# A banded attention and feed-forward kernel: the third tile's attention values in runs of two steps, the order of the work made anew, and the ring's buffers numbered by place

## The chip, the core and the metric

The kernel runs on one core of one Trainium2 chip. The metric is the time of one execution on the device, in microseconds; the number given for a kernel is the median of its runs. The core has five engines that matter here, each with a queue of instructions of its own: TensorE (PE, matmuls into PSUM), VectorE (DVE), ScalarE (ACT), GpSimd (POOL) and SyncE (SP), which issues nearly all the DMA transfers. An instruction waits at the head of its queue until what it needs is there, and everything behind it on that queue waits with it. So the order in each queue matters as much as what is computed.

## The reference

Attention over 8 x 8 heads, 576 positions and head size 64, in which a position sees only the 64 positions that end with itself; then its output, as 4608 tokens of 512 features, goes through a feed-forward layer of 2048 hidden features.

```
scores = scale * q @ k.T
mask = (rel >= 0) & (rel < window)          # rel = query position - key position, window 64
attn = softmax(where(mask, scores, -1e9))
x = (attn @ v), heads side by side           # [4608, 512]
h = x @ w_in                                 # [4608, 2048]
g = where(h >= 1, h, where(h <= -1, 0, (h + 1) ** 2 / 4))
out = g @ w_out                              # [4608, 512]
```

All of it is float32. A large matmul is made of three, each number being split in a high part and a rest: high by high, rest by high, high by rest.

## The kernel before, in words

**Tiles.** The 4608 tokens are 9 tiles of 512. The first three (PLAIN = 3) are computed directly: for each of 16 slices f of 128 hidden features, `ffn_in` (line 933) makes h in 12 matmuls, the activation follows, and `ffn_out` (line 984) adds to the output in 12 matmuls. The other six tiles form three supers of two tiles. For a super, the first layer is done with seven products in place of eight (the table PARTS, after Strassen), for eight groups n of two slices each: `ffn_product` (line 862) is 6 matmuls, and the results are put together in the h tiles by `h_copy` (line 280 in the profile, the common copy) and `h_add` (line 877). The sums of weights for the products are made once, kept in DRAM (`kept`), and loaded again for each product into a ring of six buffers (`ring_load`, line 843). In the first half of a super the first tile's outputs are made beside the products; the second tile's h goes out to DRAM (`spill`, line 880) for six of the eight groups and comes back (line 884) in the second half, where only outputs are made.

**The activation** of one slice is five instructions on tiles of 128 x 512: relu on ACT (line 946), square on ACT or DVE (lines 951 and 953), the gate on DVE (line 958: min with 1, max with h, both inputs in SBUF where h comes from the h tiles), the cast to the high part on ACT (line 963), and the low part on DVE or POOL (line 968). The pools of `a`, `gh` and `gl` have two buffers each. Outputs that have been summed up are copied and stored (line 1013); two of the four stores of a super's first tile go out from an h tile (`out<-h`), since the h tile is free by then.

**Attention** is 36 steps of 128 tokens. Each has scores on TensorE (line 425) into the two banks of the PSUM pool ps_a, mask and scale (442), maximum (446), exponential (453), inverse (460, 461), normalisation (465) and transposes (472), and then values on TensorE (line 507), which are split into xh (282 or 280) and xl (520). In the supers the values of two steps are one run into both banks of ps_a. In the third plain tile, steps 8 to 11, the scores of a step and the values of the step before it are one piece of work on TensorE, the values into a bank of ps_h. That piece is named `joined` in the code.

**What sets the order.** Class Plan is a list scheduler that runs while the program is written. Every piece of work has a key, a cost in ns per engine that may do it, what it needs, and which buffers of which pool it takes and gives back. At each step, each engine looks at what could start within PATIENCE ns of its earliest, and takes the smallest key of that; the earliest start over the engines is then written. Costs and keys come from a table of numbers at the head of the file. Work marked `shared` on DVE and all work on POOL are kept apart in the plan (`held`). The plan isn't what the chip does: it only fixes which instruction stands behind which on each queue, and, where two engines may do a piece, which of them does.

## Time and profile before

| what | value |
|---|---|
| time, median of 3 runs | 871.41 us (871.04 to 872.35) |
| the profiled execution | 871.15 us, span 869.4 us |
| granted TensorE clock | 1.00 |
| matmuls | 6718 |
| HBM read / written | 112.86 MB / 33.55 MB |

The span goes from the first to the last thing that the profiler saw; the execution's time has 1.75 us more around it. Rows of a group read: line, engine, operation, output <- inputs, shape, count, then busy time in us and mean ns of one, then how long the engine was idle just before such instructions and what ended that. Rows of a timeline read: start in us, length in us, engine, line, operation, count, and in brackets an idle time with what ended it. A matmul's end is modelled, so that single ones seem to overlap with the next; starts are what counts. The trace counts each matmul of scores and values twice (x64 and x32), where the order has 32 and 16.

### The profile page before, as it was taken

To read this page: it belongs to the slowest core of one execution; us is meant where nothing else is said; L and a number is where in the kernel's file an instruction comes from. 1 tells how busy PE (TensorE), PEld (TensorE's weight loads), DVE (VectorE), ACT (ScalarE), POOL (GpSimd) and SP (SyncE) were. 2 spreads that over 40 slices of the span, in tenths; PEclk is the share of its full clock that TensorE was granted. 3 is DMA by queue.
4 is the path that set the end of the run, shared out by engine and by line. 5 is a ranking of instruction groups with operands and counts; after the bars stand their busy time and mean duration, and the time that the engine had idled before them with its cause. 6 is when DMAs were issued, how large, how long until landed. Compare 5 with 4: busy or idle time off the path is not lost.

```text
span 869.4 us, 17790 instructions
## 1 busy us (share of the span) xinstructions
PE 857.3 (99%) x6718; PEld 699.7 (80%) x6718; DVE 652.2 (75%) x1260; ACT 490.5 (56%) x1236; POOL 208.7 (24%) x230
## 2 busy tenths in 40 slices
PE   8899999999999999999999999999999999999998
PEld 6788888888788887777878888888888888888786
DVE  6999995989887868888878969877789734343452
ACT  6999966556664566433447755343457633322564
POOL 1000045557542732131214001222141011111000
PEclk9999999999999999999999999999999999999999
DMA  8992126768644215766664418666544054635221
GB/s 317 413 393 77 49 80 217 218 184 250 195 161 142 83 37 176 243 207 194 196 205 135 176 43 267 204 197 212 171 134 146 25 177 145 194 126 182 74 97 48
DMA packets 88373, 147.58 MB, mean 170 GB/s; under 512 B 7776, under 2 KB 36704, under 8 KB 88288
## 3 DMA queue, kind: packets, MB, share of 16 engines
q1 hardware_dynamic: 87856, 145.40, 51.1%
q8 instruction: 53, 0.87, 0.4%
q10 hardware_dynamic: 432, 1.05, 0.4%
q14 instruction: 32, 0.26, 0.1%
HBM read 112.86 MB, written 33.55 MB: 168 GB/s over the span
## 4 chain that ended last, share of the span: by engine, by line
PE 91%; DVE 4%; DMA 3%; ACT 1%; issue 1%; SPq 0%; ACTq 0%
PE acc L984 44%; PE ps_h L862 24%; PE ps_h L933 15%; PE ps_a L425 3%; PE ps_a L507 3%; DMA raw<-in_w 2%; DVE ptd L472 1%; DVE h L877 1%; DMA kt<-in_k 1%; ACT sm L453 1%; DVE a L958 1%; PE ps_h L507 0%; PE ps_a L493 0%; DVE a L953 0%; DVE nm L446 0%
## 5 line engine op out<-in xcount | busy, mean ns | idle before, releaser
L984 PE MATMUL acc<-wts,gh 128*128 128x512 f32 x1152 | 358.2, 392 | 0.0
L984 PEld LDWEIGHTS acc<-wts,gh 128*128 128x128 f32 x1152 | 213.9, 188 | 45.9 <-issue 0.3
L984 PE MATMUL acc<-wts,gl 128*128 128x512 f32 x576 | 224.5, 390 | 0.0
L968 POOL TENSOR_TENSOR gl<-a,gh 128x512 fp32r<-128x512 f32 (+1 forms) x81 | 104.6, 1292 | 400.9 <-ACT gh L963 316.1
L862 PE MATMUL ps_h<-wts 128*128 128x512 f32 x720 | 182.3, 393 | 0.7 <-DVE h L877 0.5
L862 PEld LDWEIGHTS ps_h<-wts 128*128 128x128 f32 x720 | 133.4, 188 | 32.5 <-DVE h L877 3.8
L472 DVE STREAM_TRANSPOSE ptd<-sm 32x256 f32<-32x256 f32 x336 | 146.4, 436 | 7.8 <-PE ps_a L507 1.6
L946 ACT ACTIVATE a<-h 128x512 f32<-128x512 f32 x96 | 60.6, 632 | 136.2 <-DVE h L877 98.7
L877 DVE TENSOR_TENSOR h<-h,ps_h 128x512 f32<-128x512 f32 x120 | 82.3, 685 | 70.4 <-PE ps_h L862 66.8
L933 PE MATMUL ps_h<-xh,wts 128*128 128x512 f32 (+1 forms) x424 | 129.7, 374 | 1.3 <-DVE a L958 0.9
L984 PEld LDWEIGHTS acc<-wts,gl 128*128 128x128 f32 x576 | 108.1, 188 | 23.0 <-DVE gl L968 0.2
L453 ACT ACTIVATE sm<-sm,nm 128x96 f32<-128x96 f32 (+1 forms) x256 | 93.1, 366 | 41.0 <-DVE nm L446 40.9
L963 ACT CAST gh<-a 128x512 fp32r<-128x512 f32 (+1 forms) x149 | 89.3, 600 | 47.6 <-DVE a L958 27.4
L958 DVE SCALAR_TENSOR_TENSOR a<-a,h 128x512 f32<-128x512 f32 x96 | 79.4, 827 | 29.4 <-ACT a L951 27.4
L933 PEld LDWEIGHTS ps_h<-xh,wts 128*128 128x128 f32 x424 | 77.4, 188 | 16.8 <-DVE a L958 1.3
L933 PE MATMUL ps_h<-xl,wts 128*128 128x512 f32 (+1 forms) x212 | 78.5, 370 | 0.6 <-DVE xl L520 0.6
L951 ACT ACTIVATE a<-a 128x512 f32<-128x512 f32 (+1 forms) x121 | 74.4, 615 | 3.6
L862 PE MATMUL ps_h<-xs,wts 128*128 128x512 f32 x288 | 73.9, 392 | 0.1
L862 PEld LDWEIGHTS ps_h<-xs,wts 128*128 128x128 f32 x288 | 53.7, 188 | 11.9 <-ACT h L280 0.5
L280 ACT COPY h<-ps_h 128x512 f32<-128x512 f32 x42 | 24.6, 586 | 68.3 <-PE ps_h L862 68.2
L968 DVE TENSOR_TENSOR gl<-a,gh 128x512 fp32r<-128x512 f32 (+1 forms) x68 | 45.0, 663 | 8.9 <-ACT gh L963 8.0
L946 ACT ACTIVATE a<-ps_h 128x512 f32<-128x512 f32 (+1 forms) x53 | 29.3, 553 | 33.4 <-PE ps_h L933 32.2
(108 smaller groups left out, 856.7 us busy)
## 6 DMA issues: line engine op xcount, KB each, us to landing
wts<-kept SPq DMA_DIRECT2D x168, 256.0 KB, 3.0
vt<-in_v SPq DMA_DIRECT2D x72, 256.0 KB, 3.7
kt<-in_k SPq DMA_DIRECT2D x35, 384.0 KB, 4.3
raw<-in_w SPq DMA_DIRECT2D x12, 1023.8 KB, 10.2
qt<-in_q SPq DMA_DIRECT2D x36, 256.0 KB, 3.3
spill<-h SPq DMA_DIRECT2D x18, 512.0 KB, 3.0
h<-spill SPq DMA_DIRECT2D x18, 512.0 KB, 3.6
out<-o SPq DMA_DIRECT2D x27, 256.0 KB, 2.6
```

The lines of the kernel that those rows point to most:

```text
L425: nc.tensor.matmul(banks[h][r, p, :n], lhsT=qt[half[h], p, r], rhs=kt[half[h], p, i * m:i * m + n], start=not masked, stop=not masked or p ...
L453: nc.scalar.activation(sm[:, p, :], (ps if masked else sm)[:, p, :], AF.Exp, bias=nm[:, p:p + 1], scale=scale if masked else 1.0, accum_ou ...
L472: nc.vector.transpose(dst[:, :, r], src[:, :, c * SQ:(c + 1) * SQ])
L862: nc.tensor.matmul(ps, lhsT=r[:, part, cp], rhs=x_op(k, xp)[:, cp], start=j in (0, 1, 3, 4) and i == 0 and cp == 0, stop=j in (1, 2, 5, 6) ...
L877: nc.vector.tensor_tensor(out=h[:, to], in0=h[:, of], in1=prods[u, n, b], op=ALU.add)
L933: nc.tensor.matmul(ps, lhsT=wts[f, 0][:, part, c * P:(c + 1) * P], rhs=x[:, c, r], start=(c == 0 and j == 0), stop=(c == NP - 1 and j == 2),)
L946: nc.scalar.activation(gs[t, f, r.start][0], phs[t, f, r.start], AF.Relu, bias=0.5, scale=0.5)
L951: nc.scalar.activation(a, a, AF.Square)
L958: nc.vector.scalar_tensor_tensor(out=a, in0=a, scalar=1.0, in1=ps, op0=ALU.min, op1=ALU.max)
L963: nc.scalar.copy(g[1], g[0])
L968: engine[eng].tensor_tensor(out=g[2], in0=g[0], in1=g[1].bitcast(F32), op=ALU.subtract)
L984: nc.tensor.matmul(acc[t, i], lhsT=g[:, sub], rhs=wts[f, 1][:, part], start=(q == 0 and j == 0), stop=(q == NF - 1 and j == 2),)
```

## The change

Three things are changed.

First, in the third tile the scores of a step stand alone on TensorE, and the values of two steps (8 and 9, 10 and 11) are one run into both banks of ps_a, as the supers already do it. The `joined` pieces and the dictionary that carried them are gone. One flag, `paired`, now says for every step whether it waits for the next or ends a pair.

Second, the table has new numbers: keys of attention (B_DUE, B_STEP, B_FIRST, A_END, A_SUPER), of the products and outputs (C_STEP, Q_STEP, O_AFTER, O_LATER, O_CHANGE, G_LEAD, B_LATER), of the weights' sums (S_LATE, S_LATER, S_PACE), of reloads (R_LEAD, H_LEAD), of building the supers' inputs (BUILD), two costs (VV_PE, TURN) and POOL's PATIENCE.

Third, `ring_load` numbers the ring's buffers by a product's place i in the order, not by the product j. The two differ where LAST_PARTS swaps two products, in the last group of each super.

```
-PATIENCE = dict(ACT=300, DVE=0, Pool=404, PE=0, SP=0)
+PATIENCE = dict(ACT=300, DVE=0, Pool=176, PE=0, SP=0)
...
-G_LEAD = -1.3
-B_LATER = 6.43
+G_LEAD = -3.65
+B_LATER = 9.9
...
-        joined = SOON <= s and i < TILES[t] // SB - 1 and t < PLAIN
+        paired = (i < 4, i >= 4) if t >= PLAIN else (i % 2 == 0, i % 2 == 1) if s >= SOON else (False, False)
...
-        if before:
-            sv, (needs_v, gives_v, split) = before.popitem()
-
-            def do(e):
-                att_scores(s, masked, ps)
-                att_values(sv, "ps_h")
-
-            xs = add(
-                key, dict(PE=B_PE), do, needs + needs_v, takes=[ps, ps, "sm", "ps_h"],
-                gives=[("qt", xq), ("kt", xk)] + gives_v,
-            )
-            split(xs, key, "ps_h")
-        else:
-            xs = add(
...
+        xs = add(
+            key, dict(PE=S_LATER_PE if s >= SOON else S_PE[near(s)] + 500 * masked), lambda e: att_scores(s, masked, ps), needs,
+            takes=[ps, ps, "sm"], gives=[("qt", xq), ("kt", xk)],
+        )
...
-            x = add(due, dict(DVE=608), lambda e: att_low(t, i), [x], gives=[(pv, xo, t >= PAIRED and i >= 4)])
+            x = add(due, dict(DVE=608), lambda e: att_low(t, i), [x], gives=[(pv, xo, paired[1])])
...
-        if joined:
-            before[s] = needs, gives, split
-        elif t >= PAIRED and i < 4:
+        if paired[0]:
             waiting[s] = needs, gives, split
-        elif t >= PAIRED:
+        elif paired[1]:
...
-            xo = add(key, dict(PE=2 * V_LATER_PE - 91), both, needs0 + needs, takes=[pv, pv], gives=gives0 + gives)
+            xo = add(key, dict(PE=VV_PE), both, needs0 + needs, takes=[pv, pv], gives=gives0 + gives)
...
-    def ring_load(u, n, j):
-        m = 7 * (n + u * NF // 2) + j
+    def ring_load(u, n, i, j):
+        m = 7 * (n + u * NF // 2) + i
```

The numbers of instructions are the same on TensorE (5079 in both, the first difference at the 990th, which starts at about 163 us); on DVE, 28 squares become 11 (on ACT 111 become 128), and 62 low parts of 128 x 512 become 64 (on POOL 77 become 75). The changed file's lines are 15 lower from the products on: line 946 is 931 there, 951 is 936, 963 is 948, 884 is 869, 1013 is 998, 933 is 918, 984 is 969.

ACT's queue in the last super, in the first half, at about 800 to 812 us of the profile before. The numbers behind the names tell tiles apart: `a_8619` is the activation of one slice, and its cast is the row that reads it.

```order
L946 ACTIVATE a_8619<-h_4243 128x512
L963 CAST gh_8629<-a_8565 128x512
L946 ACTIVATE a_8664<-h_4243 128x512
L951 ACTIVATE a_8664<-a_8664 128x512
L963 CAST gh_8683<-a_8619 128x512
L280 COPY h_4244<-ps_h_8675 128x512 x2
L946 ACTIVATE a_8719<-h_4244 128x512
L963 CAST gh_8728<-a_8664 128x512
L946 ACTIVATE a_8753<-h_4244 128x512
```

The same place after the change:

```order
L931 ACTIVATE a_8621<-h_4200 128x512
L936 ACTIVATE a_8621<-a_8621 128x512
L948 CAST gh_8639<-a_8567 128x512
L931 ACTIVATE a_8666<-h_4200 128x512
L936 ACTIVATE a_8666<-a_8666 128x512
L948 CAST gh_8685<-a_8621 128x512
L280 COPY h_4201<-ps_h_8677 128x512 x2
L931 ACTIVATE a_8719<-h_4201 128x512
L936 ACTIVATE a_8719<-a_8719 128x512
L948 CAST gh_8736<-a_8666 128x512
```

Before, every other slice has its square on DVE, and there the cast of the slice before follows the relu at once; after, each relu is followed by its square on ACT, and the cast comes behind both.

SyncE's queue at the start of the first super's second half, at about 474 to 493 us before. `h_4243` and `h_4244` are the two h tiles (hA0 and hB0 in the first, hA1 and hB1 in the second), `out_0` is the output, `vt` are attention's values.

```order
L884 DMA h_4243<-spill2_101 128x1024
L403 DMA vt_5730<-in_v 128x512
L1013 DMA out_0<-o_5723 128x512
L1013 DMA out_0<-h_4244 128x512
L403 DMA vt_5757<-in_v 128x512
L403 DMA vt_5778<-in_v 128x512
L1013 DMA out_0<-h_4244 128x512
L884 DMA h_4244<-spill3_102 128x1024
L403 DMA vt_5806<-in_v 128x512
L884 DMA h_4244<-spill1_100 128x1024
L884 DMA h_4243<-spill4_103 128x1024
```

The same place after the change:

```order
L869 DMA h_4200<-spill2_101 128x1024
L998 DMA out_0<-o_5728 128x512
L998 DMA out_0<-o_5736 128x512
L998 DMA out_0<-h_4201 128x512
L403 DMA vt_5779<-in_v 128x512
L869 DMA h_4201<-spill3_102 128x1024
L998 DMA out_0<-h_4201 128x512
L869 DMA h_4201<-spill1_100 128x1024
L869 DMA h_4200<-spill4_103 128x1024
```

The second store from the h tile stood ahead of the reload of spill3 and stands behind it now; the reload of spill1, which fills the place that both stores read, comes right behind the store.

TensorE's queue at one of the third tile's steps, at about 198 to 202 us before:

```order
L984 MATMUL acc<-wts,gh 128x512 x2
L984 MATMUL acc<-wts,gl 128x512
L425 MATMUL ps_a<-kt,qt 32x96 x32
L507 MATMUL ps_h<-ptd,vt 64x64 x16
L984 MATMUL acc<-wts,gh 128x512 x2
L984 MATMUL acc<-wts,gl 128x512
```

After the change, at the first pair of the same tile:

```order
L918 MATMUL ps_h<-xh,wts 128x512
L507 MATMUL ps_a<-ptd,vt 64x64 x32
L969 MATMUL acc<-wts,gh 128x512 x2
L969 MATMUL acc<-wts,gl 128x512
L969 MATMUL acc<-wts,gh 128x512 x2
L969 MATMUL acc<-wts,gl 128x512
L969 MATMUL acc<-wts,gh 128x512 x2
L969 MATMUL acc<-wts,gl 128x512
L969 MATMUL acc<-wts,gh 128x512 x2
L969 MATMUL acc<-wts,gl 128x512
L425 MATMUL ps_a<-kt,qt 32x96 x32
```

Scores and one step's values, which stood together, are apart; the values of two steps are one run into ps_a, and the next scores, which need both banks of ps_a, follow 12 matmuls later.

More of the change, by code (lines that the diff above doesn't have):

```diff
@@ L75 @@
 V_LATER_PE = 1175
-B_PE = 2100
-B_DUE = (4.4, 4.93, -0.35)
-B_STEP = 4.23
-B_FIRST = 2.51
-A_END = 5.18
+VV_PE = 2108
+TURN = 487
+B_DUE = (4.29, 5.42, -0.21)
+B_STEP = 3.66
+B_FIRST = 2.2
+A_END = 3.7
 V_PE = 1270
@@ L90 @@
 PLAIN = 3
-PAIRED = 3
 SUPERS = 3
-C_STEP = 3.15
-Q_STEP = 1.24
-S_LATE = 1.29
-S_LATER = 4.74
-S_PACE = 3.7
-O_AFTER = 5.14
-O_LATER = -0.14
-O_CHANGE = (5.19, 4.54, 5.98)
-EARLY_2 = 2.24
-A_SUPER = ((8.56, 2.95), (19.52, 3.63))
+C_STEP = 3.62
+Q_STEP = 1.2
+S_LATE = 0.9
+S_LATER = 2.11
+S_PACE = 4.57
+O_AFTER = 6.11
+O_LATER = -1.19
+O_CHANGE = (6.5, 3.94, 5.08)
+EARLY_2 = 1.86
+A_SUPER = ((8.56, 2.72), (19.84, 3.3))
 A_ORDER = (0, 4, 1, 5, 2, 6, 3, 7)
-BUILD = (-4.15, 4.08)
+BUILD = (-4.41, 5.02)
 X_PIECES = (6, 7), (8, 9), (10, 11), (12, 13), (14, 15)
@@ L113 @@
 L_DVE = 4, 6, 8
-G_LEAD = -1.3
-B_LATER = 6.43
+G_LEAD = -3.65
+B_LATER = 9.9
 H_LOAD = 1400
-H_LEAD = -1.16
+H_LEAD = 0.16
 class Plan:
@@ L576, in banded_attention_then_ffn @@
     last = dict(s=[], t=[], v=[], j=None)
-    before, waiting = {}, {}
+    waiting = {}
     def tt(n, k=1):
@@ L638, in add_step @@
         needs = [xq, xk] + [last["r"]] * masked + last["s"]
-        if before:
-            sv, (needs_v, gives_v, split) = before.popitem()
-            def do(e):
-                att_scores(s, masked, ps)
-                att_values(sv, "ps_h")
-            xs = add(
-                key, dict(PE=B_PE), do, needs + needs_v, takes=[ps, ps, "sm", "ps_h"],
-                gives=[("qt", xq), ("kt", xk)] + gives_v,
-            )
-            split(xs, key, "ps_h")
-        else:
-            xs = add(
-                key, dict(PE=S_LATER_PE if s >= SOON else S_PE[near(s)] + 500 * masked), lambda e: att_scores(s, masked, ps), needs,
-                takes=[ps, ps, "sm"], gives=[("qt", xq), ("kt", xk)],
-            )
+        xs = add(
+            key, dict(PE=S_LATER_PE if s >= SOON else S_PE[near(s)] + 500 * masked), lambda e: att_scores(s, masked, ps), needs,
+            takes=[ps, ps, "sm"], gives=[("qt", xq), ("kt", xk)],
+        )
         last["s"] = [xs]
@@ L705, in add_step @@
                 x = add(
-                    due, dict(DVE=440), lambda e, piece=piece: att_transpose_both(s, *piece),
+                    due, dict(DVE=TURN), lambda e, piece=piece: att_transpose_both(s, *piece),
                     ready if ends else taken or x, takes=["pt2"] * (not n), gives=[("sm", xs)] * ends,
@@ L726, in split @@
                     after.append(raw_of[u, r])
-                x = add(due, dict(ACT=485, DVE=608), lambda e: x_take(s, i, e), after, takes=takes, gives=[(pv, xo, t >= PAIRED and i >= 4)])
+                x = add(due, dict(ACT=485, DVE=608), lambda e: x_take(s, i, e), after, takes=takes, gives=[(pv, xo, paired[1])])
                 if i < 4:
@@ L848, in add_ring @@
             after += [l1[PLAIN - 1, RING_PIECE + f] for f in range(3)] + sums_read[1] + sums_read[2]
-        x = add(key - R_LEAD, dict(SP=R_LOAD), lambda e: ring_load(u, n, j), after, takes=["ring"], lag=DMA_LAG)
+        x = add(key - R_LEAD, dict(SP=R_LOAD), lambda e: ring_load(u, n, i, j), after, takes=["ring"], lag=DMA_LAG)
         ring_last[:] = [x]
@@ L896, in add_products @@
             at = key + C_STEP * i / 7
-            ring = add_ring(u, n, j, at)
+            ring = add_ring(u, n, i, j, at)
             after = [ring, *x_done]
```

4 lines of the change are left out of this document (2 added, 2 removed).

## The prediction

> **What bounds the kernel now.** I read the busy line of the page first, then the chain of waits, then the timelines of TensorE, DVE, POOL and SyncE at the places where TensorE falls behind its own pace. The first fence has TensorE's line of the page; one piece of the chain of waits (start, length, what); DVE's row for the gate, which reads two tiles in SBUF; and one stretch of 25 us (busy time of PE, weight loads, DVE, ACT, POOL, then clock, DMA share, GB/s).
>
> ```profile
> PE 857.3 (99%) x6718; PEld 699.7 (80%) x6718; DVE 652.2 (75%) x1260; ACT 490.5 (56%) x1236; POOL 208.7 (24%) x230
> ...
> 474.25 36.27 PE acc L984 x159
> ...
> L958 DVE SCALAR_TENSOR_TENSOR a<-a,h 128x512 f32<-128x512 f32 x96 | 79.4, 827 | 29.4 <-ACT a L951 27.4
> ...
> 475.00:500.00 25.00, 25.00 (x112) 20.70 (x111) 24.44 (x55) 18.69 (x38) 0.35 (x1) 1.00 0.53 180
> ```
>
> TensorE is the bound, at full clock. A run of 159 large matmuls takes 36.27 us; a single one shows as 0.39 because its end is modelled, so the pitch is (36.27 - 0.39) / 158 = 0.227 us. The change takes no matmul away and adds none. So nothing can come but from matmuls that start later than the pitch allows. A group of n shows as 0.39 + (n - 1) x 0.227 when nothing holds it up, and the next one starts n x 0.227 after its start. The next fence has the places behind the first difference between the two orders (about 163 us) where this fails by 0.25 us or more; columns: start, length, what.
>
> ```profile
> 341.45 3.14 PE L862 MATMUL ps_h<-wts 128*128 128x512 f32 x12
> 351.23 2.97 PE L862 MATMUL ps_h<-wts 128*128 128x512 f32 x11
> 386.25 1.52 PE L862 MATMUL ps_h<-wts 128*128 128x512 f32 x6
> 387.85 1.66 PE L862 MATMUL ps_h<-xs,wts 128*128 128x512 f32 x6
> 390.48 0.39 PE L984 MATMUL acc<-wts,gl 128*128 128x512 f32 x1
> 391.00 3.06 PE L862 MATMUL ps_h<-wts 128*128 128x512 f32 x12
> 398.92 0.39 PE L984 MATMUL acc<-wts,gl 128*128 128x512 f32 x1
> 400.09 2.20 PE L507 MATMUL ps_a<-ptd,vt 128*64 128x64 f32 x64 [0.79 <-DVE sm L442]
> 406.21 0.39 PE L984 MATMUL acc<-wts,gl 128*128 128x512 f32 x1
> 406.77 1.65 PE L862 MATMUL ps_h<-wts 128*128 128x512 f32 x6 [0.18 <-DVE h L877]
> 807.36 0.39 PE L984 MATMUL acc<-wts,gl 128*128 128x512 f32 x1
> 808.10 1.67 PE L862 MATMUL ps_h<-wts 128*128 128x512 f32 x6 [0.35 <-DVE h L877]
> ```
>
> Worked out one by one: 341.45: 3.14 - 2.89 = 0.25. 351.23: 2.97 - 2.66 = 0.31. 387.85: due at 386.25 + 6 x 0.227 = 387.61, so 0.24, and 1.66 - 1.525 = 0.135 inside. 391.00: due at 390.71, 0.29, and 3.06 - 2.89 = 0.17 inside. 400.09: due at 399.24 (0.32 after the start before it, as 218.40 to 218.72 below), 0.85. 406.77: 0.33 and 0.125. 808.10: 0.51 and 0.145. Sum: 0.25 + 0.31 + 0.375 + 0.46 + 0.85 + 0.455 + 0.655 = 3.36 us. This is what a better order can win behind 163 us; the long idle times of the start lie in a part whose order is the same.
>
> **What is late at these places.** The last of them, and the same steps ten microseconds earlier, where they do no harm:
>
> ```profile
> 797.73 0.69 DVE L958 SCALAR_TENSOR_TENSOR a<-a,h 128x512 f32<-128x512 f32 x1
> ...
> 805.77 1.67 DVE L958 SCALAR_TENSOR_TENSOR a<-a,h 128x512 f32<-128x512 f32 x1
> 807.37 0.68 DVE L877 TENSOR_TENSOR h<-h,ps_h 128x512 f32<-128x512 f32 x1
> ```
>
> ```profile
> 798.79 1.29 POOL L968 TENSOR_TENSOR gl<-a,gh 128x512 fp32r<-128x512 f32 x1 [6.86 <-ACT gh L963]
> 805.60 1.29 POOL L968 TENSOR_TENSOR gl<-a,gh 128x512 fp32r<-128x512 f32 x1 [5.52 <-ACT gh L963]
> ```
>
> The gate (L958) takes 0.69 us when POOL is idle and 1.67 when it starts 0.17 behind a low part on POOL: it ends 0.55 after POOL's end at 806.89, as if it had waited for that end. Behind it on DVE's queue stands the addition L877, which is to free what the product at 808.10 needs. One clash costs DVE 0.98. The group's mean, 827 ns, against 0.69 is 96 x 0.137 = 13 us of DVE time lost over the kernel; most of it hits nobody, since DVE has slack outside a few stretches.
>
> **What the order changes here.** The groups by shape have, before: the square on ACT and on DVE, the cast on ACT, the low part on DVE and on POOL:
>
> ```profile
> L951 ACT ACTIVATE a<-a 128x512 f32<-128x512 f32 x111 | 70.2, 632 | 3.4
> L953 DVE TENSOR_TENSOR a<-a 128x512 f32<-128x512 f32 x28 | 19.8, 709 | 23.4 <-ACT a L946 23.2
> L963 ACT CAST gh<-a 128x512 fp32r<-128x512 f32 x139 | 85.4, 614 | 45.2 <-DVE a L958 25.1 <-PE acc L984 16.9 <-DVE den L460 2.6
> L968 DVE TENSOR_TENSOR gl<-a,gh 128x512 fp32r<-128x512 f32 x62 | 42.6, 687 | 8.9 <-ACT gh L963 8.0 <-PE acc L984 0.7
> L968 POOL TENSOR_TENSOR gl<-a,gh 128x512 fp32r<-128x512 f32 x77 | 101.5, 1318 | 397.9 <-ACT gh L963 313.2 <-PE acc L984 49.5 <-DVE ptd L472 11.9
> ```
>
> In the new order 17 of the 28 squares on DVE go to ACT, and in the products' stretches ACT's sequence becomes relu, square, cast, where at the clashes it is relu, cast (first and second fence of the change's section). At 805 the cast ended before the gate could start, so POOL had its low part first. With the square ahead of the cast on ACT, the gate may start when the square ends, and the cast then takes 0.61 more before POOL can begin: the gate is through 0.6 of its 0.69 us by then. The trace has this pattern already, at 797.73 and 798.79: gate 0.69. The cast and the low part come 0.63 later at those places; TensorE takes what POOL made at 805.60 to 806.89 only after the products from 808.10 on, over 2 us later, so this is covered. I take the whole 3.36 as won, between 0 (the clashes only move) and 3.36 and some 0.3 for excesses too small to be listed.
>
> **The third tile's attention.** Before: five visits to small matmuls (scores; three times scores and values; values). After: six (four scores, two pairs of values).
>
> ```profile
> 218.40 0.39 PE L984 MATMUL acc<-wts,gl 128*128 128x512 f32 x1
> 218.72 1.15 PE L507 MATMUL ps_a<-ptd,vt 128*64 128x64 f32 x32
> 219.80 0.73 PE L984 MATMUL acc<-wts,gh 128*128 128x512 f32 x2
> ...
> 222.74 1.00 PE L425 MATMUL ps_a<-kt,qt 64*32 64x96 f32 x64
> ...
> 241.41 2.08 PE L507 MATMUL ps_a<-ptd,vt 128*64 128x64 f32 x64
> 243.43 0.73 PE L984 MATMUL acc<-wts,gh 128*128 128x512 f32 x2
> ```
>
> A visit costs 0.32 - 0.227 = 0.09 going in and 0.73 - (0.39 + 0.227) = 0.11 coming out, 0.20. One step's values take 219.80 - 218.72 = 1.08 alone, a pair (which the later tiles have) 243.43 - 241.41 = 2.02, so two pairs save 2 x (2.16 - 2.02) = 0.28. Sum: +0.20 - 0.28, taken as -0.1.
>
> The pair now fills both banks of ps_a, which the next scores need.
>
> ```profile
> 221.12 0.69 DVE L520 TENSOR_TENSOR xl<-ps_a,xh 128x512 fp32r<-128x512 f32 x1
> ```
>
> With one bank, the last read ends at 221.81, and the scores at 222.74 come 0.93 later. A second read of 0.69 leaves about 0.2; a few transposes ahead of it on DVE eat that. I take 0.2 for both pairs, between 0 and 2 x 0.69. The Trainium skill (its first page, Trainium Kernel Development and Optimization, section Best Practices) says to mind PSUM pressure, since tiling the array speeds up the matmuls and not the emptying of PSUM. It speaks against the pair: if nothing covers the second read, this term would be 1.4 and the time 1.2 more than I say; no row of before shows the pair in this tile, so the trace can't decide.
>
> **The second halves of the first two supers.** There the h tiles of the first half are reloaded on SyncE's queue, through slots that the output stores from h must leave first. SyncE's own rows, the DMA table, and the latency of everything that goes through the spill tiles:
>
> ```profile
> 478.51 0.62 SPq L1013 DMA_DIRECT2D out<-h  x1
> 481.40 0.33 SPq L884 DMA_DIRECT2D h<-spill  x1
> 481.82 0.38 SPq L403 DMA_DIRECT2D vt<-in_v  x1
> 483.15 3.15 SPq L884 DMA_DIRECT2D h<-spill  x2
> ...
> out<-h SPq DMA_DIRECT2D x6, 256.0 KB, 3.8
> ...
> DMA to landing us min/median/max: 2.7/3.5/4.6
> ...
> 493.13 0.39 PE L984 MATMUL acc<-wts,gl 128*128 128x512 f32 x1
> ```
>
> The new order puts the second store from h behind the reload of spill3 (third and fourth fence of the change's section), so it inherits that reload's wait: about 481.82 in place of 478.51. It lands 3.8 later, 485.6; only then may spill1's reload go, which waits for it, with every later reload behind it on the queue, and it lands at 489.1 where it was issued at 483.15 before. From there relu, square, gate, cast and low part (0.63 + 0.63 + 0.69 + 0.61 + 0.69 = 3.25, and some 0.3 of hand-overs) end at 492.7; TensorE needs them at 493.13. So on medians 0.4 is left; with both transfers at 4.6 it is 0.8 + 1.1 - 0.4 = 1.5 late, and DVE is 98% busy here. I take 0.3 a super, 0.6 in all, between 0 and 3.0. In the third super the order of these four is as before. The Trainium skill (DMA: Bandwidth & Descriptors, Anatomy of one DMA — SWDGE (gpsimd) path) fits 2.0 us and the bytes at 436 GB/s to a DMA of GpSimd's queue: 2.6 for the store and 3.2 for the reload, by which nothing would wait and the time would be 0.6 lower; the rows here are 3.8 and 3.5, on another queue, and I keep to them.
>
> **The rest.** The ring's numbering differs only for the last group of each super, where two products are swapped; loads that waited for a slot by the wrong number no longer do. TensorE's waits name no ring load behind 163 us: nothing won. Two low parts more on DVE (62 to 64) cost 1.4 us of an engine that loses 17 squares (12 us). A new clash somewhere: 0.2, between 0 and 0.66, the dearest one above.
>
> **The sum.** On the profiled run, 871.15 us (span 869.4, 1.75 around it): 871.15 - 3.36 - 0.1 + 0.2 + 0.6 + 0.2 = 868.7. That run lies 0.26 below the median of 871.41, so against medians: **869.0**. Its own range is 867.5 (the last three terms and half of the 0.3 too small to list fall away: 1.15, and the pairs save 0.3) to 869.9 (the reloads at half of their upper bound, 1.5 in place of 0.6).
>
> **Rivals.** First, the reloads are late in both supers: 1.2 each in place of 0.3, so 869.0 + 1.8 = 870.8. For it: the queue order, and DVE at 24.44 of 25 us. Against: the medians leave 0.4. Second, the change doesn't do what its order suggests: gates and low parts meet elsewhere, as often and as harmfully; 871.15 - 0.1 + 0.26 = 871.3. For it: POOL keeps 75 of 77 low parts. Against: only seven places hurt before, all with ACT's cast ahead of the square or a mask behind the gate. Third, slower: DVE becomes the bound in the second halves. It has 25 - 24.44 = 0.56 us to spare per 25 us at 475. If the new order puts both new low parts (0.69 each) and one clash (0.98) into such a stretch, TensorE waits 2.36 - 0.56 = 1.8 a super; in three supers 5.4, so 869.0 + 5.4 = 874.4. It decides as soon as DVE's work there grows by over 0.56. Against: DVE loses nine times as much as it gains (12 us against 1.4), though mainly in the products' stretches.
>
> **How the numbers follow.** The forecast 0.70, late reloads 0.12, clashes that move 0.10, DVE bound 0.08. A measurement of this kernel can tell 0.2%, 1.74 us, from no change: faster is below 869.67. Of the forecast's 0.70, about 0.04 lies above that. So faster 0.66, same 0.04 + 0.12 + 0.10 = 0.26, slower 0.08. The range takes the forecast and the late reloads: 867.5 to 870.9.
>
> **What would show it.** Right: gates L958 with mean near 0.72 in the supers' product stretches; no gap at the products that took the place of 391, 406 and 808; spill1's reload landing within 0.4 us of need. Wrong: gates still at 1.7 with product groups over their pitch; second-half runs of out matmuls broken by a wait for gl, which names the reloads if ACT's relu waited for a DMA, and DVE if relu waited for DVE; scores of the third tile waiting for xl.

## The result, and the profile after

The changed kernel takes 867.04 us (median of 4 runs, 866.73 to 868.34), the kernel before, in the same runs, 871.8 (871.04 to 872.35): a ratio of 0.9949, with a 95% interval of 0.9932 to 0.9966, so about 4.4 us less. The forecast was 869.0 (2.4 less) with a range from 867.5: the direction was right, the size was not. The profiled execution of the changed kernel is one of 867.07 us, with a span of 865.3, against 871.15 and 869.4. The line of busy time, and the groups of the gate, the cast on ACT and the low part on POOL:

```profile
PE 854.4 (99%) x6718; PEld 699.8 (81%) x6718; DVE 636.7 (74%) x1258; ACT 501.9 (58%) x1247; POOL 192.5 (22%) x221
...
L943 DVE SCALAR_TENSOR_TENSOR a<-a,h 128x512 f32<-128x512 f32 x96 | 67.3, 701 | 36.3 <-ACT a L936 34.4
```

```profile
L948 ACT CAST gh<-a 128x512 fp32r<-128x512 f32 x139 | 85.7, 616 | 65.0 <-PE acc L969 44.7 <-DVE a L943 18.3 <-DVE u L544 1.5
L953 POOL TENSOR_TENSOR gl<-a,gh 128x512 fp32r<-128x512 f32 x75 | 97.3, 1298 | 434.0 <-ACT gh L948 434.0
```

The gate's mean went from 827 ns to 701: the long gates are gone but for three (0.89 to 1.08 us). The row to look at is the cast: it now sat idle for 44.7 us until TensorE freed a buffer (`PE acc`), where before it was 16.9. That hints at an activation that runs further ahead of TensorE; the experiments say how far this sum can be trusted.

TensorE ran on the places where it had stalled. Three stretches of 25 us, before and then after (PE's busy time is the second number):

```profile
375.00:400.00 25.00, 24.10 (x222) 18.39 (x220) 21.86 (x39) 9.32 (x27) 4.06 (x3) 1.00 0.56 175
400.00:425.00 25.00, 24.73 (x220) 19.87 (x221) 18.90 (x37) 11.45 (x42) 4.71 (x4) 1.00 0.69 220
800.00:825.00 25.00, 24.65 (x109) 20.07 (x108) 11.12 (x15) 12.24 (x22) 1.38 (x2) 1.00 0.30 107
```

```profile
375.00:400.00 25.00, 25.00 (x225) 20.46 (x224) 20.83 (x39) 12.05 (x40) 5.01 (x4) 1.00 0.74 235
400.00:425.00 25.00, 25.00 (x230) 20.15 (x229) 20.92 (x44) 10.55 (x32) 3.86 (x3) 1.00 0.65 210
800.00:825.00 25.00, 25.00 (x112) 20.69 (x111) 11.71 (x18) 15.19 (x26) 1.28 (x1) 1.00 0.25 85
```

Going through all of TensorE's starts of the changed kernel, no matmul behind 163 us starts more than 0.12 late, and those 0.11 are what each return from the small matmuls costs. All of the 3.36 us is gone. The last pieces of the two chains of waits tell the whole difference, since the last 228 matmuls are the same in both:

```profile
813.87 51.69 PE acc L984 x228
```

```profile
809.75 51.69 PE acc L969 x228
```

They start 4.12 us earlier. Of this, 0.41 is there already at a place that the change can't have moved: a run of values at 80 us, where no engine's order differs yet (the first difference is on DVE, at 136 us).

```profile
80.08 1.08 PE ps_a L507 x32
```

```profile
79.67 1.08 PE ps_a L507 x32
```

So 0.41 is the start, which differs from execution to execution, and 3.36 are the stalls on the prediction's list. What is left is 0.35. The pairs make 0.08 of it by the prediction's prices (0.28 saved, 0.20 for one visit more). Another 0.12 lies inside the run of values at 400.09, which takes 2.20 us where the one at 241.41 takes 2.08; the list has only its late start. The other 0.15 are delays too short for the list, and rounding.

### The profile page after: what moved, and what is told of

The parts are those of the page before. It is cut to its first block, busy times and chain, and to the rows that moved or that the text cites. A ratio compares the mean times of both kernels' runs of the same rounds, so it can differ in the third digit from the quotient of the medians.

```text
span 865.3 us, 17804 instructions
## 1 busy us (share of the span) xinstructions
PE 854.4 (99%) x6718; PEld 699.8 (81%) x6718; DVE 636.7 (74%) x1258; ACT 501.9 (58%) x1247; POOL 192.5 (22%) x221
## 4 chain that ended last, share of the span: by engine, by line
PE 96%; DMA 1%; ACT 1%; DVE 1%; SPq 0%; issue 0%
PE acc L969 46%; PE ps_h L847 27%; PE ps_h L918 15%; PE ps_a L507 4%; PE ps_a L425 3%; DMA kt<-in_k 1%; DMA vt<-in_v 1%; ACT sm L453 0%; PE ps_a L493 0%; ACT u L332 0%; PE ps_h L485 0%; DVE wts L348 0%; ACT ptd L280 0%; ACT raw L309 0%; DVE sm L465 0%
## 5 line engine op out<-in xcount | busy, mean ns | idle before, releaser
L953 POOL TENSOR_TENSOR gl<-a,gh 128x512 fp32r<-128x512 f32 (+1 forms) x79 | 100.3, 1270 | 436.6 <-ACT gh L948 436.4
L847 PE MATMUL ps_h<-wts 128*128 128x512 f32 x720 | 179.1, 392 | 0.0
L948 ACT CAST gh<-a 128x512 fp32r<-128x512 f32 (+1 forms) x149 | 89.6, 602 | 67.4 <-PE acc L969 44.7
L943 DVE SCALAR_TENSOR_TENSOR a<-a,h 128x512 f32<-128x512 f32 x96 | 67.3, 701 | 36.3 <-ACT a L936 34.4
L918 PEld LDWEIGHTS ps_h<-xh,wts 128*128 128x128 f32 x424 | 77.4, 188 | 16.9 <-DVE a L943 1.3
L936 ACT ACTIVATE a<-a 128x512 f32<-128x512 f32 (+1 forms) x138 | 85.1, 617 | 4.3
```

What stands on the lines that cost most here:

```text
L847: nc.tensor.matmul(ps, lhsT=r[:, part, cp], rhs=x_op(k, xp)[:, cp], start=j in (0, 1, 3, 4) and i == 0 and cp == 0, stop=j in (1, 2, 5, 6) ...
L918: nc.tensor.matmul(ps, lhsT=wts[f, 0][:, part, c * P:(c + 1) * P], rhs=x[:, c, r], start=(c == 0 and j == 0), stop=(c == NP - 1 and j == 2),)
L936: nc.scalar.activation(a, a, AF.Square)
L943: nc.vector.scalar_tensor_tensor(out=a, in0=a, scalar=1.0, in1=ps, op0=ALU.min, op1=ALU.max)
L948: nc.scalar.copy(g[1], g[0])
L953: engine[eng].tensor_tensor(out=g[2], in0=g[0], in1=g[1].bitcast(F32), op=ALU.subtract)
```

## The experiments

Every run is a kernel of its own, with its time beside the kernel before on the same chip. A long gate is one over 1 us (15 before, 2 after). Stalls are those behind 163 us of 0.2 or more; their size is a start minus the pitch behind the start before it, from TensorE's timeline.

| run | median (before) | ratio, 95% interval | long gates | stalls: place and us |
|---|---|---|---|---|
| before | | | 15 | 388 0.24, 391 0.29, 400 0.86, 407 0.34, 808 0.51 |
| after | 867.04 (871.8) | 0.9949, 0.9932 to 0.9966 | 2 | none |
| sq_act | 870.04 (871.13) | 0.9987, 0.9978 to 0.9996 | 10 | 399 1.00, 406 0.32 |
| lows_behind_gates | 869.84 (871.46) | 0.9983, 0.9974 to 0.9992 | 4 | 391 0.29, 400 0.45, 407 0.35 |
| low_on_dve | 876.75 (871.08) | 1.0064, 1.0051 to 1.0077 | 0 | twelve, 0.25 to 1.24, the longest at 353 |
| sq_dve_again | 869.82 (871.13) | 0.9983, 0.9974 to 0.9992 | 2 | 491 1.09, 673 0.84 |
| sq_dve_products | 867.65 (871.46) | 0.9959, 0.9946 to 0.9972 | 2 | none |
| outs_earlier_56 | 868.22 (871.46) | 0.9968, 0.9955 to 0.9980 | 11 | 490 0.25, 805 0.56 |
| outs_earlier_54 | 867.04 (871.46) | 0.9955, 0.9943 to 0.9968 | 1 | none |
| after_old_steps | 869.43 (871.18) | 0.9979, 0.9970 to 0.9988 | 18 | 458 0.54, 640 0.54, 806 0.51 |
| before_turn487 | 871.92 (871.18) | 1.0004, 0.9994 to 1.0015 | 13 | 176 0.52, 196 1.23, 197 to 201 2.56, 810 0.51 |
| after_turn440 | 870.49 (871.18) | 0.9993, 0.9984 to 1.0002 | 4 | 195 0.64, 219 1.23, 413 0.73 |
| after_turn475 | 868.30 (871.18) | 0.9962, 0.9949 to 0.9974 | 0 | 202 0.44 |
| pairs_old_table | 871.80 (871.13) | 1.0011, 1.0002 to 1.0020 | 12 | 174 0.92, 179 0.30, 192 0.82, 241 0.21, 312 0.59, 353 0.40, 809 0.51 |
| joined_new_table | 869.33 (871.13) | 0.9984, 0.9975 to 0.9992 | 2 | 175 0.60, 176 0.79, 351 0.26 |
| store_first | 866.83 (871.08) | 0.9952, 0.9939 to 0.9964 | 2 | none |
| spill1_later | 872.79 (871.08) | 1.0015, 1.0006 to 1.0024 | 2 | 491 0.93, 674 0.96, 837 2.22 |
| ring_only | 871.50 (871.08) | 1.0003, 0.9994 to 1.0011 | 15 | as before, and 196 0.21 |

### Is the clash what stalls TensorE, and is it the square's place that removes it?

Two kernels that keep the old order and remove the clash, each from one side. In the first, squares move; in the second, the low parts that met a long gate.

```
 # sq_act: the list of work as the plan of the kernel before wrote it, the last six tiles
-relu (ACT), ..., square (DVE), gate (DVE)
+relu (ACT), square (ACT), ..., gate (DVE)          # 24 squares
 # lows_behind_gates: 11 low parts
-low part (POOL) at its place, gate (DVE)
+gate (DVE), low part (DVE)
```

> The kernel before with its order as it was on TensorE, POOL and SyncE, but the 24 squares that the six last tiles had on DVE are on ACT, each right behind its relu. If the clash of gate and POOL's low part makes the stalls (my theory), gates over 1 us fall from 15 to 3 or fewer, the seven stalls behind 163 us (3.4 us) lose at least the four at 391, 400, 407 and 808 (2.4 us), and the time is 2.0 to 3.4 us below the kernel before. If the new table wins by its other moves (rival), the time stays within 0.7 us of before. If the pairs in the third tile win it (rival), it stays too.

> The kernel before with its order kept, but the 11 low parts on POOL that its trace shows beside a long gate are on DVE instead, each right behind that gate; squares stay where they were. If the clash makes the stalls, those 11 gates take 0.69 (the four long gates at 425, 473, 607 and 655, beside other POOL work, stay), the stalls at 391, 400, 407 and 808 (2.4 us) shrink to under 0.5 together, and the time is 1.5 to 2.5 us below before. If the stalls at 400 and 407 come from the attention's own order (rival), only 391 and 808 go: 0.7 to 1.2 us below. If the clash harms nobody, none.

They win 1.1 and 1.5 us by their ratios. The first was to win 2.0 to 3.4; the second was to leave under 0.5 of the stalls at 391, 400, 407 and 808, and leaves 1.09. In the last super, sq_act takes all six clashes away and the stall at 808 goes; those at 388 and 391 go too. In the first super it has four long gates of up to 1.77 us. At three places of these (361, 380 and 397 us) the square was on ACT before already, so the square's place can't free them: the gate comes late on DVE, and POOL has begun. In lows_behind_gates every meeting that it takes up is gone, and the stall at 808 and that at 388 with it. But at 391 and 407 it is as before, and at 400 half is left. There the kernel with no clash shows DVE with hardly a pause from 394 to 400 (start, length):

```profile
395.54 0.88 DVE L472 STREAM_TRANSPOSE ptd<-sm 32x256 f32<-32x256 f32 x2
396.45 0.69 DVE L877 TENSOR_TENSOR h<-h,ps_h 128x512 f32<-128x512 f32 x1
397.17 0.44 DVE L472 STREAM_TRANSPOSE ptd<-sm 32x256 f32<-32x256 f32 x1
397.62 0.69 DVE L958 SCALAR_TENSOR_TENSOR a<-a,h 128x512 f32<-128x512 f32 x1
398.23 0.68 DVE L968 TENSOR_TENSOR gl<-a,gh 128x512 fp32r<-128x512 f32 x1
398.93 0.44 DVE L472 STREAM_TRANSPOSE ptd<-sm 32x256 f32<-32x256 f32 x1
399.40 0.56 DVE L442 SCALAR_TENSOR_TENSOR sm<-ps_a,later 128x384 f32<-128x384 f32 x1
```

The mask (L442) that must empty ps_a for TensorE's next values is simply the last of a full queue of transposes, additions and gates. So by this run the clash made the stalls at 388 and 808 and at least half of that at 400 (a clash alone need not cost anything: in sq_act the gate at 380 is long and the stall at 388 is gone). One of the queue's rows is there through the edit: the low part at 398.23 was on POOL before, and holds DVE for 0.70 us. Without it the mask would come that much earlier and the 0.45 left at 400 would be gone, an estimate; so the clash's share there lies between 0.41 and all of it. The stalls at 391 and 407 are a queue that is packed too tightly. The kernel low_on_dve takes the clash away more bluntly:

```
 # low_on_dve: in the first tile of each super, same places
-low part (POOL)
+low part (DVE)
```

> The kernel before with the low parts that POOL makes for the first tile of each super on DVE instead, at the same places of the order; squares stay on DVE. This takes the clash away by its other side: POOL has nothing to read beside those gates. Clash theory: gates of 1.3 us or more are gone there, and the stalls at 391, 407 and 808 too, but DVE has 44 more instructions of 0.69 in its queue, which may delay additions and masks where attention is dense: 0 to 3 us faster than before. If ACT's order alone matters (rival: the cast's place, not the clash), no gain.

No long gate is left, and it is 0.64% slower, where 0 to 3 us faster was expected: 46 more instructions of 0.69 us where DVE was the engine that is waited for. Removing a clash by giving DVE more work costs more than the clash.

Then the other way round: the changed kernel with squares back on DVE.

```
 # sq_dve_again: 24 slices that the kernel before had on DVE (19 of them on ACT after the change)
-relu (ACT), square (ACT), ..., gate (DVE)
+relu (ACT), ..., square (DVE), gate (DVE)
 # sq_dve_products: only the 15 of these that lie in the products' stretches
```

> The changed kernel with only one thing undone: the squares of the 24 slices that the kernel before had on DVE are on DVE again, right ahead of their gates, so that ACT's cast follows the relu at once there. Clash theory: gates of 1.3 us or more come back at ten or more places, and the time is 1.0 to 3.5 us above the changed kernel, though not all places need hurt, since the products have other neighbours now. If the other moves of the table win it, it is within 0.7 us of the changed kernel, whether gates are long or not.

> The changed kernel with 15 squares of the products' stretches on DVE, as the kernel before has them, and those of the second halves left alone. The run that moved both kinds lost 2.8 us, and its trace has no stall in the products' stretches, only at 490 and 673, in the second halves. So by that trace: no long gate comes back, and the time is the changed kernel's within 0.4 us. By the theory of my prediction (the square's place on ACT removes the clash): ten long gates and 1 to 3 us.

No clash comes back in either, where ten or more were expected of the first. What sq_dve_again loses, it loses in the second halves, where squares on DVE come into the chain behind the reloads; with those left alone, sq_dve_products has no stall and 0.9959 against the changed kernel's 0.9949, intervals that overlap. So the square's place, on which my prediction built, removes the clash in the last super of the old order (sq_act), and in the new order the clash stays away without it. The three engines of sq_dve_products in the last super, by DVE, ACT, POOL:

```profile
787.88 0.69 DVE L938 TENSOR_TENSOR a<-a 128x512 f32<-128x512 f32 x1
788.60 0.69 DVE L943 SCALAR_TENSOR_TENSOR a<-a,h 128x512 f32<-128x512 f32 x1
```

```profile
788.41 0.62 ACT L948 CAST gh<-a 128x512 fp32r<-128x512 f32 x1 [1.18 <-PE acc L969]
```

```profile
789.11 1.33 POOL L953 TENSOR_TENSOR gl<-a,gh 128x512 fp32r<-128x512 f32 x1 [6.82 <-ACT gh L948]
```

The square is on DVE and the cast stands right behind the relu on ACT, just as before the change. But the cast waits 1.18 us for TensorE to be done with the gh buffer. So POOL starts 0.51 behind the gate, not 0.17 ahead of it.

In the last super the changed kernel has both, the square on ACT and a cast that waits (0.52 us at 802.76), and by these runs either alone is enough. In the first super the square's place can't be the difference, as it is on ACT in sq_act and in the changed kernel alike. Square, cast, low part and gate there at about the same time, in sq_act and then in the changed kernel:

```profile
395.14 0.63 ACT L951 ACTIVATE a<-a 128x512 f32<-128x512 f32 x1
...
395.68 0.61 ACT L963 CAST gh<-a 128x512 fp32r<-128x512 f32 x1
...
396.36 1.30 POOL L968 TENSOR_TENSOR gl<-a,gh 128x512 fp32r<-128x512 f32 x1 [6.10 <-ACT gh L963]
...
396.50 1.71 DVE L958 SCALAR_TENSOR_TENSOR a<-a,h 128x512 f32<-128x512 f32 x1
```

```profile
393.44 0.63 ACT L936 ACTIVATE a<-a 128x512 f32<-128x512 f32 x1
...
394.49 0.63 ACT L948 CAST gh<-a 128x512 fp32r<-128x512 f32 x1 [0.42 <-PE acc L969]
...
394.55 0.69 DVE L943 SCALAR_TENSOR_TENSOR a<-a,h 128x512 f32<-128x512 f32 x1
395.20 1.30 POOL L953 TENSOR_TENSOR gl<-a,gh 128x512 fp32r<-128x512 f32 x1 [6.70 <-ACT gh L948]
```

Two things differ: the cast waits 0.42, and DVE comes to the gate 0.48 us behind the square's end, not 0.73. Without the wait the low part would start at 394.66, an estimate by the steps of sq_act (0.54 from the square's start to the cast's, 0.68 from the cast's to the low part's). That is still 0.11 behind the gate. So a gate that DVE reaches promptly would be enough here too, by little, and the wait makes it safe. No run takes away the wait alone, so which of the two the changed kernel needs stays open.

### Is it the lead over TensorE?

If the activation runs further ahead of the outputs, both gh buffers are full when the cast's turn comes, and cast and low part are held until after the gate. The two numbers that set the lead are C_STEP and O_AFTER.

```
 # outs_earlier_56                      # outs_earlier_54
-O_AFTER = 6.11                        -O_AFTER = 6.11
+O_AFTER = 5.6                         +O_AFTER = 5.4
 # after_old_steps
-C_STEP = 3.62
+C_STEP = 3.15
-O_AFTER = 6.11
+O_AFTER = 5.14
```

> The changed kernel with one number changed: first-half outputs are planned 0.51 earlier behind their products (O_AFTER 5.6 in place of 6.11), and the order is made anew. In this order the cast no longer has to wait for TensorE to free a gh buffer, so POOL's low part starts ahead of the gate again. Lead theory (the new order wins since the activation runs further ahead of TensorE's outputs, so that cast and low part are held back until the gate has begun): ten or more gates of about 1.67 us come back in the products' stretches of the three supers, most without harm; with the one stall near 804 as the kernel before had it, 0.5 to 1.0 us above the changed kernel. If the squares' engine decides it, no clash comes back where the square is on ACT.

> Control to the run with 5.6: the same number set to 5.4. The order that comes out has the casts held by TensorE again, so no clash, by the lead theory, and the time is the changed kernel's within 0.4 us. If it is the number itself that counts (earlier outputs mean less cover), it is at least as slow as the run with 5.6.

> The changed kernel with the old C_STEP and O_AFTER (3.15 and 5.14 in place of 3.62 and 6.11), nothing else. Lead theory: the clashes come back at 14 or more places in the products' stretches, of which only those at the end of each super's products hurt, about 0.5 us each near 457, 638 and 804: 1.0 to 2.0 us above the changed kernel; no stall between 384 and 430. If these two numbers carry the whole change, 3 us and more.

The long gates came out as the lead theory said in all three: eleven, one and 18. The times fit less well: by the ratios outs_earlier_56 is 1.6 us and after_old_steps 2.6 us above the changed kernel, where 0.5 to 1.0 and 1.0 to 2.0 were expected; outs_earlier_54 is the same, as expected.

These orders are made anew, and a second thing changes with them: 37, 28 and 30 squares are on DVE, where the changed kernel has 11. All eleven long gates of outs_earlier_56 and 15 of the 18 of after_old_steps have their square on DVE, right ahead of them. So these two runs don't tell the lead from the square's place. Only sq_dve_products does: its squares are on DVE, its casts wait, and no gate of those is long.

With 5.6 one of the eleven stalls TensorE, by the same chain as before the change (DVE, then TensorE):

```profile
802.58 1.72 DVE L943 SCALAR_TENSOR_TENSOR a<-a,h 128x512 f32<-128x512 f32 x1
804.22 0.68 DVE L862 TENSOR_TENSOR h<-h,ps_h 128x512 f32<-128x512 f32 x1
```

```profile
804.95 1.42 PE L847 MATMUL ps_h<-wts 128*128 128x512 f32 x5 [0.40 <-DVE h L862]
```

With 5.4, still earlier, one long gate and the changed kernel's time: it isn't how early the outputs are, but what order comes of it, and whether gate and low part meet in it. The sum of the cast's waits for TensorE doesn't tell this by itself: it is 64.2 us with 5.4, but 44.1 with 5.6 where the changed kernel has 44.7. The single rows do: with 5.6 the cast in front of the long gate waits for nothing,

```profile
801.73 0.60 ACT L948 CAST gh<-a 128x512 fp32r<-128x512 f32 x1
```

where the cast of sq_dve_products at 788.41 waited 1.18. With both old numbers there are 18 long gates, and of these three hurt, the last of each super's products:

```profile
458.12 0.73 PE L847 MATMUL ps_h<-wts 128*128 128x512 f32 x2 [0.38 <-DVE h L862]
...
640.29 0.50 PE L847 MATMUL ps_h<-wts 128*128 128x512 f32 x1 [0.38 <-DVE h L862]
...
806.37 0.50 PE L847 MATMUL ps_h<-wts 128*128 128x512 f32 x1 [0.35 <-DVE h L862]
```

Each costs about 0.53, 1.6 in all, and nothing stalls between 384 and 430 us. So the clashes come and go with these two numbers, and the stalls at 391 to 407 depend on something else.

### What packed DVE's queue at 391 to 407?

One of the costs that the change corrects is that of a transpose of the later attention (TURN). There are eight to a step, on DVE.

```
 # before_turn487: the kernel before
-                    due, dict(DVE=440), lambda e, piece=piece: att_transpose_both(s, *piece),
+                    due, dict(DVE=487), lambda e, piece=piece: att_transpose_both(s, *piece),
 # after_turn440                        # after_turn475
-TURN = 487                            -TURN = 487
+TURN = 440                            +TURN = 475
```

> The kernel before with one number changed: a pair of transposes costs 487 ns in the plan, not 440 (the trace has 436 for one by itself, with a start to start of about 0.45 in a run of them). The order is made anew. If the stalls at 387 to 407 come from a plan that packs the attention's transposes too tightly on DVE, they go, the clash in the last super stays with its one stall (0.5 to 0.7 us near 804), and the time is 1.8 to 2.8 us below before. If they come from the clash or from the keys, they stay: within 0.8 us of before.

> The changed kernel with the transposes' cost in the plan back at 440 ns, nothing else. Packing theory: stalls of DVE's work come back between 384 and 430 us, 1.5 to 4 us in all, and some long gates too. If the keys carry it, within 0.5 us of the changed kernel.

> The changed kernel with the transposes' cost at 475 ns, a try at a version that is better than both: an order without long gates and with the same work. As TensorE has no stall left behind 163 us in the changed kernel, it can only win what is lost at the visits to small matmuls: the changed kernel's time within 0.4 us.

In before_turn487 TensorE runs through both stretches where the old kernel lost 1.17 us, though two gates of 1.35 and 1.73 us stand there (at 393 and 410):

```profile
375.00:400.00 25.00, 25.00 (x231) 20.18 (x229) 21.77 (x40) 8.69 (x26) 7.44 (x8) 1.00 0.64 199
400.00:425.00 25.00, 25.00 (x225) 20.46 (x224) 19.83 (x37) 9.52 (x28) 4.36 (x4) 1.00 0.70 231
```

So the stalls at 388 to 407 go with this one number here, and long gates are harmless there once the queue has room. But the whole order is made anew, and another remake does the same: pairs_old_table, in the next part, keeps 440 and has no stall between 354 and 808. So the rows show that the queue was packed; that the cost of 440 packed it isn't shown. The time was missed: the kernel is no faster, since the new order stalls in the third tile's attention, 4.3 us at 176, 196 and 197 to 201 (the last with a lower clock, see the end). In the changed kernel, 440 brings back stalls, but only one of them between 384 and 430: 0.73 at 413, where 1.5 to 4 were expected, by an addition that comes late as at 391 and 407, here behind a gate of 1.71 us and six transposes. The others, around 195 and 219, are in the third tile. 475 gives an order with no long gate at all and is no better than 487: one low part on POOL comes 0.44 late in the third tile, and it is 0.13% (1.1 us) slower than the changed kernel by the two ratios, where 0.4 us was expected at most; the intervals overlap. Nothing tried beats the changed kernel by more than the runs differ.

### The third tile's pairs

```
 # pairs_old_table: the code of the pairs, the table and the ring's numbering of before
+        paired = (i < 4, i >= 4) if t >= PLAIN else (i % 2 == 0, i % 2 == 1) if s >= SOON else (False, False)
 # joined_new_table: the new table and the ring's numbering, the code that joins
+        joined = SOON <= s and i < TILES[t] // SB - 1 and t < PLAIN
```

> The kernel before with the third tile's values in pairs and nothing else (its table stays, the ring's numbering too; the order is made anew from that). Working by visits: 0.1 us less on TensorE in the third tile, everything else by chance of the new order, since the squares stay where the old keys put them: within 1 us of the kernel before. If the pairs are what wins (rival), 3 to 4 us below it.

> The changed kernel with the third tile's scores and values joined as before, the new table and the ring's numbering kept. Working by visits: 0.1 us more in the third tile than the changed kernel, and otherwise as it, so within 0.7 us. If the pairs win, 3 to 4 us above it. A miss by 1 us or more either way with stalls outside the third tile would say that the table fits only the work that it was searched for.

The pairs alone give nothing, as expected: 0.11% slower. The stalls at 388 to 407 are gone with the order that comes of them, and 3 us of others have come between 174 and 312. Joined with the new table it was a miss: 0.35% or 3 us slower than the changed kernel by the ratios, not within 0.7; its stalls make 1.65 us of that. The two larger ones are where the third tile's attention runs, at 175 and 176 (this kernel's lines are two above those of the kernel before):

```profile
174.95 0.73 PE L986 MATMUL acc<-wts,gh 128*128 128x512 f32 x2 [0.43 <-ACT gh L965]
176.31 0.50 PE L986 MATMUL acc<-wts,gl 128*128 128x512 f32 x1 [0.62 <-POOL gl L970]
```

ACT has a whole exponential (eight activations, 168.79 to 171.68) ahead of the relu that these outputs need. So the new keys fit the pairs, and neither is worth its share alone. Whether keys can be found with which the joined pieces do as well wasn't tried.

### The reloads, and the ring

```
 # store_first (SyncE, first two supers)        # spill1_later (SyncE, all supers)
+out <- h, second store                          h <- spill3
 h <- spill3                                     out <- h, second store
-out <- h, second store                         -h <- spill1
 h <- spill1                                     h <- spill4
 h <- spill4                                    +h <- spill1
```

> The changed kernel with the second output store from the h tile ahead of spill3's reload again, in the first two supers, nothing else moved. My prediction gave this order 0.3 us a super of cost. If reloads cost anything, this is 0.2 to 0.6 us faster; if the margins of 0.1 and 0.2 us that the changed kernel's trace shows at the first matmul that needs spill1's work hold, the time is the same within 0.3 us and those margins grow by 1 us or more.

> The changed kernel with the reload of spill1 behind that of spill4 on SyncE's queue in every super, nothing else moved. Spill1 lands 0.4 us (its issue alone) to 2 us (the other transfer goes first) later. If the reload chain is on the edge, as the margins of 0.1 and 0.2 us say, TensorE stalls at that place in the first two supers by the delay less the margin, so 0.2 to 1.8 us each: 0.4 to 3.6 us slower. If there is cover that I don't see, it is the same.

> The kernel before with only the ring's numbering changed; the order of all queues is the same. No wait of TensorE behind 163 us names a ring load, so all theories expect the time of before, within 0.3 us. It also shows how much the first 50 us, whose instructions are the same in all these kernels, vary between executions.

The new order does what the prediction said of SyncE (changed kernel; SyncE's rows, the relu that waits for spill1, its low part, and the matmul that takes it):

```profile
477.24 0.33 SPq L869 DMA_DIRECT2D h<-spill  x1
477.62 0.42 SPq L998 DMA_DIRECT2D out<-h  x1
481.89 7.22 SPq L869 DMA_DIRECT2D h<-spill  x3
```

```profile
485.55 0.63 ACT L931 ACTIVATE a<-h 128x512 f32<-128x512 f32 x1 [1.30 <-DMA h<-spill]
```

```profile
488.68 0.68 DVE L953 TENSOR_TENSOR gl<-a,gh 128x512 fp32r<-128x512 f32 x1
```

```profile
489.55 0.40 PE L969 MATMUL acc<-wts,gl 128*128 128x512 f32 x1
```

Spill1's reload leaves SyncE 4.27 us behind the store and the relu waits for it, but the low part ends 0.19 us ahead of its matmul (0.10 in the second super). With the store first, that reload leaves right behind spill3's and the time is the same (the low part is then 1.30 us ahead); with it one place later, TensorE waits at just this point in all supers:

```profile
490.94 0.73 PE L969 MATMUL acc<-wts,gh 128*128 128x512 f32 x2 [0.51 <-ACT gh L948]
...
836.70 0.73 PE L969 MATMUL acc<-wts,gh 128*128 128x512 f32 x2 [1.80 <-ACT gh L948]
```

That the edge is there was right; that anything is lost on it was not. The two supers that I had named lose 1.9 us together, within what was expected; the third, which I had not named, loses 2.2. The ring's numbering is worth nothing, as expected.

## Why the prediction was right and wrong

**Right:** that TensorE is the bound and only late starts can be won; which starts these are, and that all 3.36 us of them go; the pairs' small gain; the ring; the place and the order of the reload chain.

**The step that failed in size: the three costs added to the sum.** "+ 0.2 + 0.6 + 0.2" for the second bank of ps_a, the reloads and a new clash measured 0. The second reads of xl in the changed kernel end 1.8 and 0.7 us ahead of the scores, where I had 0.2 left; the reloads were in time by 0.10 and 0.19; the two clashes left hurt nobody. Each had a bound of zero below, and I took a middle value of each: three risks that are each more likely than not to cost nothing were summed as if they would all come. Without them the sum is 867.7 on the profiled run. The other 0.6 to the measured 867.07 are the start (0.41), which I took as fixed although the same instructions run there at different speed in each execution, and 0.2 that the list of stalls had left out, 0.12 of it inside the values at 400. The range's lower end, 867.5, held no room for a start that differs, and so it missed by 0.46. The risk itself was real: in after_turn440, an order made of the same work, scores do wait for xl.

```profile
218.52 0.35 PE L425 MATMUL ps_a<-kt,qt 64*32 64x96 f32 x2 [0.78 <-DVE xl L520]
```

**The step that failed in its mechanism: "With the square ahead of the cast on ACT, the gate may start when the square ends".** This holds in the last super (sq_act). In the first super it can't be the reason, since the square was on ACT at 361, 381 and 397 before already and the gates were long: there DVE came 0.7 to 1.1 us late to the gate. And in the new order the gates stay short without it: with those squares back on DVE the cast waits for TensorE to free its buffer and holds POOL back. The prediction had neither, DVE's late gates nor the wait. The cast's row stood in the prediction, and I read only its duration, not its idle time and what ended it.

**And "I take the whole 3.36 as won" by the clash:** about half of it isn't the clash's, and that this part went as well was luck, as far as the prediction goes. The clash accounts for the stalls at 388 and 808 and for 0.41 to 0.85 of that at 400, 1.4 to 1.9 us in all. Those at 391 and 407 are a queue on DVE in which attention's transposes stand too densely; that at 400 has both, this queue and the clash at 397. Those at 391 and 407 stay when the clash goes (lows_behind_gates) and all go when long gates stay (before_turn487); that at 391 also goes when squares leave DVE's queue (sq_act). I had looked at DVE's long gates and not at the six us of rows around the mask in which DVE never pauses. The small delays at 341 and 351, 0.56 in sum, no run takes apart.

**The rivals:** the late reloads came only where a run made them later; the clashes did not move elsewhere; DVE in the second halves did not become the bound, but sq_dve_again shows how near it is: four squares more there cost 1.9 us of stalls.

The parts don't add up, since each undone alone costs more than half the gain: the ratios of after_old_steps, after_turn440 and joined_new_table lie 0.30, 0.44 and 0.35% above the changed kernel's, together 1.1% where the change won 0.5. By their stalls it is 1.6, 2.6 and 1.65 us, 5.8 where 3.36 were to be won. An order is good only as a whole: take one number back, and the scheduler writes a different one.

## What to carry to other kernels

A bounding engine that is 99% busy is worked on by listing its late starts one by one, and every one of them has its own queue behind it; one that names the same releaser need not have the same cause. Where two engines block each other, ask what holds back the second of them: a buffer that the bound engine frees late can order them for nothing. And in a sum, a risk that has zero as its lower end and cover in sight belongs in the range, not in the middle. Last, a run in which a scheduler makes the order anew changes more than the number that is edited: count what else moved before giving that number the credit.

## What the runs showed of the hardware

Whichever of the gate on DVE and the low part on POOL starts second pays. A gate that starts 0.17 us behind the low part takes 1.67 us instead of 0.69. A low part that starts 0.48 behind the gate (sq_act, at 790) takes 1.35 instead of 1.28; little, as the gate is nearly through:

```profile
790.55 1.35 POOL L968 TENSOR_TENSOR gl<-a,gh 128x512 fp32r<-128x512 f32 x1 [6.24 <-ACT gh L963]
```

The Trainium skill (SBUF — State Buffer, Who interferes with whom) has this rule: a DVE instruction with two inputs in SBUF and a GpSimd instruction that reads SBUF exclude each other, and the order of issue decides which of them is blocked. These rows agree on which one waits; the gate at 805.77 ends 0.55 us behind POOL's end, a little less than its whole 0.69.

Two waits close together can cost more than themselves. In before_turn487 TensorE starts 1.23 us late at 195.84, behind a wait for ACT, and 0.85 late at 197.25, behind one for POOL. Then the granted clock falls (clock is the number behind POOL's):

```profile
195.00:197.00 2.00, 0.73 (x2) 0.30 (x2) 1.95 (x6) 1.75 (x3) 1.08 (x1) 1.00 0.71 211
197.00:199.00 2.00, 1.75 (x4) 1.46 (x5) 1.94 (x5) 0.00 (x0) 1.76 (x5) 0.57 0.04 8
199.00:201.00 2.00, 2.00 (x6) 1.52 (x6) 1.91 (x5) 0.90 (x2) 1.96 (x3) 0.57 0.09 28
```

Matmuls start 0.427 apart there, not 0.227, for about 3 us, which costs another 1.7. Single waits elsewhere did without, at a clock of 1.00 all through: 0.86 at 400 in the kernel before, 1.24 at 353 in low_on_dve. What exactly brings the clock down, no run here takes apart.

The first 80 us have the same instructions on TensorE in all 18 profiles, and yet the run of values that starts at 80.08 in the kernel before starts at 79.44 in outs_earlier_54 and at 81.89 in ring_only. A single profile of this kernel can't tell a change of 1 or 2 us by its span; the stalls by place can.
